# Partition-major model and MLP width in a two-layer decode kernel: long weight runs, strided weight columns, x and result in column form

## The chip, the cores and the metric

The kernel runs on one core of a Trainium2 chip. The time is the device time of one execution in microseconds (us), as the median of several executions; the profile's span, from its first to its last instruction, is some 2 us shorter than that time. Every timed kernel was run beside the kernel before, on the same chip. In the views, PE is the matmul engine and PEld its weight loads, DVE and ACT are the vector and the scalar engine, and SPq is the sequencer that issues the loads and stores of the one queue.

## The reference

One token passes twice through attention over the last 4,096 cached positions (32 heads of 192) and then through an MLP block. All tensors are bf16. The model width D is 640, the MLP width F is 1,536. Cut to what matters:

```python
def _A_ref(x, k_cache, v_cache, wq, wo):        # x: [1, 1, 640]
    q = (x @ wq)                                # wq: [640, 32 * 192]
    p = softmax(q k^T * 192 ** -0.5)            # k, v: the last 4096 positions of each head
    return (p v) @ wo                           # wo: [32 * 192, 640]

def _B_ref(x, w1, w2, w3, w4):                  # one token: the shifted part (w1, w2) is zero
    x1 = x
    h2 = gelu(layernorm(x1) @ w3) @ w4          # w3: [640, 1536], w4: [1536, 640]
    return x1 + h2

x = A_x
for _ in range(2):
    x = x + _A_ref(layernorm(x), ...)
    x = x + _B_ref(layernorm(x), ...)
```

## The kernel before

The kernel is a stream of 1.5 MB loads (a head of K or V at a time), all on one DMA queue, into 11 buffers ("cells") of 12 KB per partition. It keeps vectors as columns: D = 640 is a tile of 128 partitions by 5 columns. Which d stands where is the subject of the change. Before, column n holds d = 128 n + p on partition p:

```python
def load_wq(layer, kc):
    nc.sync.dma_start(wq_sb[:, kc, :], A_wq[kc * P:(kc + 1) * P, :])

def load_w3(layer):
    src = B_w3.rearrange("(k p) f -> p k f", p=P)                 # runs of one row, 3,072 B
    ...
def load_w4(layer):
    pairs = B_w4.rearrange("(k p two) n -> p k (two n)", p=P, two=2)  # runs of two rows, 2,560 B
    ...
# attention's output projection: 128 neighbouring columns of wo are the weights
nc.tensor.matmul(y_ps[:, n:n + 1], lhsT=wo_t[:, k * D + n * P:k * D + (n + 1) * P], rhs=oT[:, k:k + 1], ...)
# MLP: every second column of w3, 128 neighbouring columns of w4
f0 = 2 * P * (fc // 2) + fc % 2
nc.tensor.matmul(hp[:, i:i + 1], lhsT=w3[kc][:, f0:f0 + 2 * P - 1:2], rhs=xc[:, kc:kc + 1], ...)
nc.tensor.matmul(y2_ps[:, n:n + 1], lhsT=w4[fc][:, n * P:(n + 1) * P], rhs=hT[:, fc:fc + 1], ...)
# the end: turn [128, 5] into [5, 128], store five runs of 256 B
nc.tensor.transpose(row_ps[:, :], x4[:, :], Eq[:].rearrange("p j b -> p (j b)"))
nc.vector.tensor_copy(o_fin, row_ps[:])
nc.sync.dma_start(out.rearrange("a b (n p) -> (a b n) p", p=P), o_fin)
```

Every such matmul has one column as its moving operand, and with it goes a weight load of 128 x 128 (104 ns in the trace, overlapped, so that a pair of load and matmul starts every 27 ns). When layer 1 begins, 9 of the 11 cells hold data that is kept from layer 0. The first two V loads of layer 1 must therefore wait for the cells of w3 and w4 of layer 0.

Of the kernel before, what the change touches and what calls it, by code (L numbers as in the profile page):

```python
# [17 lines left out]
P = 128  # L18
# [17 lines left out]
def kernel(  # L36
# [37 lines left out]
    NA = Dh // 32  # L74
    NKX = 6
    NKEEP, NCELL = 7, 11
    WARM = 66



# [1 line left out]
    assert NA * D + FREE - 2 * VW <= FREE  # L82

    W3C, W4C = FREE // F, FREE // D
    assert W4C % 2 == 1 and W4C < NF
    GROUPS = [[list(range(h, h + QH)) for h in range(0, H, QH)] for _ in range(2)]
    GROUPS[0].reverse()

# [32 lines left out]

    def load_x():

        x_bf = wx_sb[0:ND, 4 * P:5 * P]
        nc.sync.dma_start(x_bf, A_x.rearrange("a b (n p) -> (a b n) p", p=P))
        return x_bf

    def load_k(layer, h):
# [23 lines left out]
            V, i = kx, i - (FREE - VN)  # L152
        return V[:, i:i + n]

    def load_wq(layer, kc):
        nc.sync.dma_start(wq_sb[:, kc, :], A_wq[kc * P:(kc + 1) * P, :])
        return wq_sb

    def load_wo(layer, c):
# [9 lines left out]
    def load_w3(layer):  # L169

        t = take(("w3", layer))
        src = B_w3.rearrange("(k p) f -> p k f", p=P)
        n = W3C if layer == 0 else W3C // 2
        for k in range(0, W3C, n):
            nc.sync.dma_start(t[:, k * F:(k + n) * F].rearrange("p (k f) -> p k f", f=F), src[:, k:k + n, :])
        if layer == 0:
            nc.sync.dma_start(wx_sb[:, 0:(ND - W3C) * F].rearrange("p (k f) -> p k f", f=F), src[:, W3C:, :])
        return ([t[:, k * F:(k + 1) * F] for k in range(W3C)]
                + [wx_sb[:, k * F:(k + 1) * F] for k in range(ND - W3C)])

    def load_w4(layer):

        t = take(("w4", layer))
        blocks = [t[:, k * D:(k + 1) * D] for k in range(W4C)]
        x0 = (ND - W3C) * F
        blocks += [wx_sb[:, x0 + k * D:x0 + (k + 1) * D] for k in range(NF - W4C)]
        pairs = B_w4.rearrange("(k p two) n -> p k (two n)", p=P, two=2)
        ones_ = B_w4.rearrange("(k p two) n -> p k two n", p=P, two=2)
        h = W4C // 2
        n = h if layer == 0 else h // 2  # L190
        for k in range(0, h, n):
            nc.sync.dma_start(t[:, 2 * k * D:2 * (k + n) * D].rearrange("p (k n) -> p k n", k=n), pairs[:, k:k + n, :])
        nc.sync.dma_start(blocks[2 * h], ones_[:, h, 0, :])
        if layer == 0:
            nc.sync.dma_start(blocks[2 * h + 1], ones_[:, h, 1, :])
            rest = NF // 2 - h - 1
            nc.sync.dma_start(wx_sb[:, x0 + D:x0 + D + 2 * rest * D].rearrange("p (k n) -> p k n", k=rest),
                              pairs[:, h + 1:, :])
        return blocks

    LOADERS = {"x": load_x, "k": load_k, "v": load_v, "wq": load_wq, "wo": load_wo, "w3": load_w3, "w4": load_w4}
# [39 lines left out]
        seq.append(("w4", layer))  # L241
        return seq

    stream = [("wq", 0, 0), ("x",)] + [("wq", 0, kc) for kc in range(1, ND)] + layer_stream(0) + layer_stream(1)
    pos = [0]

    def need(*key):
# [59 lines left out]
    for i in range(WARM):  # L307
        nc.tensor.matmul(warm_ps[:], lhsT=Eq[:, 0, :], rhs=Eq[:, 0, :], start=(i == 0), stop=(i == WARM - 1))

    x_rf = wx_sb[0:ND, 6 * P:8 * P].bitcast(F32)  # L310
    nc.vector.tensor_copy(x_rf, x_bf)
    xT = const.tile([P, ND], F32, name="xT0")
    xT_ps = psm.tile([P, ND], F32, tag="psm")
    nc.tensor.transpose(xT_ps[:, :], x_rf, ident[0:ND, 0:ND])
    rs0 = const.tile([P, 1], F32, name="rs0")
    nc.vector.tensor_scalar(out=xT[:], in0=xT_ps[:], scalar1=1.0, scalar2=None, op0=ALU.mult,
                            op1=ALU.add, accum_out=rs0[:, 0:1])


# [60 lines left out]
    def qproj_steps(c, xc, part=None, row=None):  # L380


        held = {}
        n = QT if part is None else QT // 2
        t0 = c * QT + (part or 0) * n

        def project():
            need("wq", 0, ND - 1)
            if row is not None:
                N = QC // 2  # L390
                qr_ps = psm.tile([33, N], F32, tag="psm")
                for kc in range(ND):
                    for i in range(2):
                        nc.tensor.matmul(  # L394
                            qr_ps[32 * i:32 * i + 1, :], lhsT=xc[:, kc:kc + 1],
                            rhs=wq_sb[:, kc, t0 * P + i * N:t0 * P + (i + 1) * N],
                            start=(kc == 0), stop=(kc == ND - 1))
                for i in range(2):
                    nc.scalar.copy(row[32 * i:32 * i + 1, :], qr_ps[32 * i:32 * i + 1, :])
                return  # L400
            qT_ps = psm.tile([P, n], F32, tag="psm")
            for tl in range(n):
                t = t0 + tl
                for kc in range(ND):
                    nc.tensor.matmul(  # L405
                        qT_ps[:, tl:tl + 1], lhsT=wq_sb[:, kc, t * P:(t + 1) * P], rhs=xc[:, kc:kc + 1],
                        start=(kc == 0), stop=(kc == ND - 1))
            held["q"] = qT_ps

        def spread():  # L410
            if row is not None:
                qT_ps = psm.tile([P, n], F32, tag="psm")
                for tl in range(n):
                    i, j = divmod(tl, n // 2)
                    nc.tensor.matmul(qT_ps[:, tl:tl + 1], lhsT=row[:, j * P:(j + 1) * P],
                                     rhs=Eq[0:33, i, 0:1], start=True, stop=True)
                held["q"] = qT_ps
            Xq = big.tile([P, n, 4], BF16, name="Xq")
            nc.vector.tensor_tensor(  # L419
                out=Xq[:], in0=held["q"][:, :].unsqueeze(2).broadcast_to([P, n, 4]),  # L420
                in1=maskq[:, :].unsqueeze(1).broadcast_to([P, n, 4]), op=ALU.mult)
            held["x"] = Xq

        def repeat():
            Qrep_ps = psm.tile([P, 4 * n], F32, tag="psm")
            nc.tensor.matmul(Qrep_ps[:], lhsT=Lb[:], rhs=held["x"][:].rearrange("p t b -> p (t b)"),  # L426
                             start=True, stop=True)
            held["r"] = Qrep_ps

        def block():  # L430
            nh = n * P // Dh
            h0 = 4 * (t0 - c * QT) // NCOL
            diag = Qblk[:, c % 2].rearrange("p (h r) -> p h r", h=QH)[:, h0:h0 + nh, 0:QHEAD]
            nc.vector.tensor_tensor(
                out=diag.rearrange("p h (f x) -> p h f x", x=QW)[:, :, :, 0:NM],
                in0=held["r"][:, :].rearrange("p (h f) -> p h f", h=nh).unsqueeze(3).broadcast_to([P, nh, NCOL, NM]),
                in1=blkm[:, :].unsqueeze(1).unsqueeze(1).broadcast_to([P, nh, NCOL, NM]), op=ALU.mult)

        return project, spread, repeat, block
# [149 lines left out]
    def out_proj(layer, *terms):  # L589
# [3 lines left out]
        for i, (c, oT, n, k) in enumerate(order):  # L593
            wo_t = need("wo", layer, c)
            nc.tensor.matmul(
                y_ps[:, n:n + 1], lhsT=wo_t[:, k * D + n * P:k * D + (n + 1) * P], rhs=oT[:, k:k + 1],
                start=(i == 0), stop=(i == len(order) - 1))
        for c, _ in terms:
            if (layer, c) == (0, 0):
# [26 lines left out]

    def turn_row(acc):
        y_ps = psm.tile([P, ND], F32, tag="psm")
        N = D // 2
        for n in range(ND):  # L630
            a, b = n * P, (n + 1) * P
            for i in range(2):
                lo_, hi = max(a, i * N), min(b, (i + 1) * N)
                if lo_ < hi:
                    nc.tensor.matmul(y_ps[lo_ - a:hi - a, n:n + 1], lhsT=acc[:, lo_ - i * N:hi - i * N],
                                     rhs=ident[0:33, 32 * i:32 * i + 1], start=True, stop=True)
        return y_ps

    def attention(layer, x_cur, rs_cur, x_new, z_new, rs_new, ss_new):
# [218 lines left out]
    def mixer(layer, x_cur, z, rs_cur, ss_cur, x_new, rs_new):  # L858
# [33 lines left out]
        for ks in kcs:  # L892
            for half, hp in enumerate(h_ps):
                order = ([(i, kc) for kc in ks for i in range(HF)] if ks is kcs[0] else
                         [(i, kc) for i in range(HF) for kc in ks])
                for j, (i, kc) in enumerate(order):
                    fc = half * HF + i
                    f0 = 2 * P * (fc // 2) + fc % 2
                    nc.tensor.matmul(
                        hp[:, i:i + 1], lhsT=w3[kc][:, f0:f0 + 2 * P - 1:2], rhs=xc[:, kc:kc + 1],  # L900
                        start=(ks is kcs[0] and j == 0), stop=(ks is kcs[-1] and j == len(order) - 1))
        give(("w3", layer))
        for half, hp in enumerate(h_ps):
# [20 lines left out]
        y2_ps = psm.tile([P, ND], F32, tag="psm")  # L924
        fcs = list(range(NF))
        if layer == 1:
            n = W4C // 4 * 2
            fcs = fcs[:n] + fcs[W4C:] + fcs[n:W4C]
        order = [(n, fc) for fc in fcs for n in range(ND)]
        for i, (n, fc) in enumerate(order):  # L930
            nc.tensor.matmul(
                y2_ps[:, n:n + 1], lhsT=w4[fc][:, n * P:(n + 1) * P], rhs=hT[:, fc:fc + 1],
                start=(i == 0), stop=(i == len(order) - 1))
        give(("w4", layer))
        if rs_new is None:
# [12 lines left out]
    attention(1, x2, rs2, x3, z[1], zs[2], zs[3])  # L948
    mixer(1, x3, z[1], zs[2], zs[3], x4, None)

    row_ps = psm.tile([ND, P], out.dtype, tag="psm")
    nc.tensor.transpose(row_ps[:, :], x4[:, :], Eq[:].rearrange("p j b -> p (j b)"))
    o_fin = Lb[0:ND, :]
    nc.vector.tensor_copy(o_fin, row_ps[:])
    nc.sync.dma_start(out.rearrange("a b (n p) -> (a b n) p", p=P), o_fin)


# [28 lines left out]
```

## Time and profile before

| what | value | view |
|---|---|---|
| time | 525.22 us, median of 3 (524.87 to 526.0) | results |
| span | 522.9 us | page |
| DMA | 415 GB/s; one queue has 99.0% of the engines' time | page |
| PE, DVE busy | 63%, 56% | page |

The lines of the page for the kernel before. The GB/s row has 40 slices of the span, 13.1 us each.

```profile
span 522.9 us, 9589 instructions
...
GB/s 345 429 424 425 423 426 427 423 424 423 427 421 428 424 422 428 423 423 423 423 399 398 388 425 427 424 424 423 426 423 424 426 423 426 421 427 425 420 410 237
DMA packets 23949, 217.08 MB, mean 415 GB/s; under 512 B 2532, under 2 KB 3044, under 8 KB 8420
```

The stream runs at some 424 GB/s nearly throughout; slices 20 to 22 (261 to 300 us), around the change of layers, are lower. So what is not hidden under the stream is there, at the start and at the end. The layer boundary before, from the timeline (start, duration, engine, line, operation, count, and in brackets the idle time before it and what ended it):

```profile
285.28 0.78 PE L899 MATMUL V_ps<-xc,cell_2751 128*128 128x1 bf16 x24
...
285.92 0.78 PE L899 MATMUL O_ps<-xc,cell_2751 128*128 128x1 bf16 x24
...
286.73 0.33 SPq L143 DMA_DIRECT2D cell_3122<-in_A_v_cache_dram  x1
...
288.32 1.43 PE L931 MATMUL y_ps<-hT,cell_2863 128*128 128x1 bf16 x45 [1.30 <-DVE gu L907]
...
289.78 0.33 SPq L143 DMA_DIRECT2D cell_3124<-in_A_v_cache_dram  x1
...
294.19 0.33 SPq L130 DMA_DIRECT2D cell_3126<-in_A_k_cache_dram  x1
```

Here w3's matmuls (line 899) end and the first V load of layer 1 is issued at once, w4's matmuls (line 931) on their buffer end and the second one is issued. The spacing of matmul pairs is the group's time less one matmul, over the count less one: (780 - 165) / 23 = 27 ns for w3, (1430 - 165) / 44 = 29 ns for w4, whose group holds one pause of 0.1 us (its other pairs start 27 ns apart).

What the sequencer waited for before it issued that first V load, from the view of its waits (line, who released it, us in total, times, longest):

```profile
SPq L143 <- PE O_ps L899: 3.0, 1, 3.0
```

The same stretch before, in the view by windows (start:end, length, busy time and count of PE, PEld, DVE, ACT and GpSimd, granted clock of PE, DMA share, GB/s):

```profile
285.00:290.00 5.00, 3.70 (x116) 3.55 (x117) 2.61 (x19) 1.91 (x8) 0.00 (x0) 0.50 1.01 371
290.00:295.00 5.00, 4.18 (x84) 2.96 (x87) 1.07 (x8) 0.30 (x2) 0.00 (x0) 0.50 1.02 430
```

And the end before, from the timeline:

```profile
519.20 0.81 PE L931 MATMUL y_ps<-hT,cell_5535 128*128 128x1 bf16 x25
520.04 0.16 DVE L936 TENSOR_TENSOR x_213<-base,y_ps 128x5 bf16<-128x5 f32 x1 [1.14 <-PE y_ps L931]
...
520.26 0.27 PE L952 MATMUL row_ps<-Eq,x_213 128*5 128x128 bf16 x1 [0.26 <-DVE x_213 L936]
520.57 0.21 DVE L954 COPY Lb<-row_ps 5x128 bf16<-5x128 bf16 x1 [0.36 <-PE row_ps L952]
520.81 0.30 SPq L955 DMA_DIRECT2D out_dram<-Lb  x1
```

From the last add to the issue of the store are 0.77 us, from there to the end of the span 2.1 us.

### The profile page before, as it was taken

Reading aid. Unit: us, or ns where it says so; the run is one execution under the profiler, and the core shown is the slowest. Engines: PE = TensorE matmul, PEld = TensorE weight load, DVE = VectorE, ACT = ScalarE, POOL = GpSimd, SP = SyncE. Lnnn points to the kernel's source line nnn. Section 1 sums busy time; section 2 is a strip of 40 time slices with the busy share of each in tenths; the row PEclk is TensorE's granted clock in tenths of the full one; section 3 lists DMA queues with packets and bytes.
Section 4 is the critical chain, followed back from the end, with each engine's and each line's share of the span. In section 5 each row is a group of like instructions: output and inputs, shape, how many; then the busy total and the mean of one; then the engine's idle time right before and its main releaser. Section 6 shows DMA issues by size and latency. Waiting matters only on the chain.

```text
span 522.9 us, 9589 instructions
## 1 busy us (share of the span) xinstructions
PE 330.3 (63%) x4146; PEld 195.5 (37%) x4146; DVE 294.6 (56%) x589; ACT 49.5 (9%) x175; POOL 4.0 (1%) x16
## 2 busy tenths in 40 slices
PE   2057668666665566767655866667675666647675
PEld 2023334333332333434333544334343333425344
DVE  2067656666574664556624264766576866654722
ACT  1000101010010100001011101001010101001011
POOL 2000000000000000000000000000000000000000
PEclk9995656567677776576555567657787865766755
DMA  8999999999999999999999999999999999999996
GB/s 345 429 424 425 423 426 427 423 424 423 427 421 428 424 422 428 423 423 423 423 399 398 388 425 427 424 424 423 426 423 424 426 423 426 421 427 425 420 410 237
DMA packets 23949, 217.08 MB, mean 415 GB/s; under 512 B 2532, under 2 KB 3044, under 8 KB 8420
## 3 DMA queue, kind: packets, MB, share of 16 engines
q1 hardware_dynamic: 23908, 216.48, 99.0%
q8 instruction: 32, 0.52, 0.4%
q14 instruction: 9, 0.07, 0.0%
HBM read 216.47 MB, written 0.00 MB: 414 GB/s over the span
## 4 chain that ended last, share of the span: by engine, by line
DMA 43%; PE 27%; DVE 25%; issue 2%; ACT 2%; SPq 1%; DVEq 0%; ACTq 0%
PE ST_ps L451 11%; DVE cell_3304 L375 9%; PE O_ps L567 8%; DVE cell_277 L375 8%; DMA cell_1925<-in_A_k_cache_dram 6%; DMA cell_4933<-in_A_k_cache_dram 5%; DMA cell_1629<-in_A_k_cache_dram 5%; DMA cell_1329<-in_A_k_cache_dram 5%; DMA cell_4637<-in_A_k_cache_dram 5%; DMA cell_5324<-in_A_v_cache_dram 5%; DMA cell_275<-in_A_k_cache_dram 4%; DVE o_sb L574 2%; DMA cell_2478<-in_A_v_cache_dram 2%; DMA cell_2690<-in_A_v_cache_dram 2%; DMA cell_5423<-in_B_w_dram 2%
## 5 line engine op out<-in xcount | busy, mean ns | idle before, releaser
L451 PEld LDWEIGHTS <-Qblk 128*16 128x16 bf16 x1536 | 86.1, 113 | 178.6 <-issue 151.1
L451 PE MATMUL ST_ps<-cell_277,Qblk 128*16 128x256 bf16 x600 | 70.1, 392 | 50.9 <-DVE cell_277 L375 34.3
L574 DVE STREAM_TRANSPOSE o_sb<-O_ps 128x384 f32<-128x384 f32 x64 | 37.2, 582 | 112.4 <-PE O_ps L567 112.3
L451 PE MATMUL ST_ps<-cell_3304,Qblk 128*16 128x256 bf16 x600 | 67.3, 382 | 43.5 <-DVE cell_3304 L375 28.3
L567 PEld LDWEIGHTS <-PT 128*2 128x2 bf16 x1024 | 47.2, 102 | 21.8 <-issue 11.3
L510 DVE STREAM_TRANSPOSE o_sb<-o_sb 128x256 bf16<-128x256 bf16 x16 | 7.1, 445 | 34.1 <-ACT o_sb L505 25.0
L582 ACT ACTIVATE oT<-oT_ps,rl 32x6 bf16<-32x6 f32 x40 | 10.3, 258 | 163.5 <-PE oT_ps L581 157.1
L581 PEld LDWEIGHTS oT_ps<-o_sb,Lq 128*32 128x32 f32 x160 | 13.2, 145 | 19.9 <-issue 16.1
L581 PE MATMUL oT_ps<-o_sb,Lq 128*32 128x6 f32 x160 | 13.9, 196 | 10.4 <-DVE o_sb L574 9.9
L587 ACT ACTIVATE oT<-oT_ps,rl 32x6 bf16<-32x6 f32 x24 | 6.2, 258 | 108.4 <-PE ST_ps L451 93.7
L405 PE MATMUL qT_ps<-xc,wq_sb 128*128 128x1 bf16 x210 | 7.2, 165 | 13.4 <-DMA wq_sb<-in_A_wq_dram 12.5
L419 DVE TENSOR_TENSOR Xq<-qT_ps,maskq 128x24 bf16<-128x24 f32 (+1 forms) x18 | 2.8, 157 | 18.3 <-PE qT_ps L405 18.3
L521 PE MATMUL PT_ps<-o_sb,Eq 128*32 128x32 bf16 x256 | 7.2, 237 | 9.2 <-DVE o_sb L510 4.0
L394 PE MATMUL qr_ps<-wq_sb,xc 128*1 128x384 bf16 x90 | 12.8, 433 | 0.0
L521 PEld LDWEIGHTS <-Eq 128*32 128x32 bf16 x256 | 5.5, 111 | 18.9 <-issue 18.8
L405 PEld LDWEIGHTS <-wq_sb 128*128 128x128 bf16 x210 | 6.8, 104 | 14.8 <-DMA wq_sb<-in_A_wq_dram 13.6
L502 ACT COPY nb_sb<-nb_ps 128x1 f32<-128x1 f32 x16 | 2.5, 159 | 97.6 <-PE nb_ps L499 97.6
L526 PE MATMUL l_ps<-lh,ones 128*128 128x4 f32 x32 | 8.5, 336 | 4.9 <-ACT PT L524 4.9
L499 PEld LDWEIGHTS nb_ps<-ones,o_sb 1*128 1x128 f32 x32 | 7.6, 292 | 7.4 <-issue 5.5
L526 PEld LDWEIGHTS l_ps<-lh,ones 128*128 128x128 f32 x32 | 7.1, 275 | 7.5 <-ACT PT L524 7.1
L499 PE MATMUL nb_ps<-ones,o_sb 1*128 1x1 f32 x32 | 8.9, 345 | 1.5 <-DVE o_sb L491 1.5
L426 PE MATMUL Qrep_ps<-Xq,Lb 128*128 128x24 bf16 (+1 forms) x18 | 3.2, 179 | 10.4 <-DVE Xq L419 10.1
(376 smaller groups left out, 533.2 us busy)
## 6 DMA issues: line engine op xcount, KB each, us to landing
wq_sb<-in_A_wq_dram SPq DMA_DIRECT2D x5, 1536.0 KB, 12.7
cell_275<-in_A_k_cache_dram SPq DMA_DIRECT2D x1, 1536.0 KB
cell_309<-in_A_k_cache_dram SPq DMA_DIRECT2D x1, 1536.0 KB, 26.4
cell_346<-in_A_k_cache_dram SPq DMA_DIRECT2D x1, 1536.0 KB, 27.1
cell_376<-in_A_k_cache_dram SPq DMA_DIRECT2D x1, 1536.0 KB
cell_444<-in_A_k_cache_dram SPq DMA_DIRECT2D x1, 1536.0 KB, 30.8
cell_503<-in_A_v_cache_dram SPq DMA_DIRECT2D x1, 1536.0 KB, 30.8
cell_505<-in_A_k_cache_dram SPq DMA_DIRECT2D x1, 1536.0 KB, 30.8
```

The costliest lines, as they stand in the source:

```text
L375: nc.vector.transpose(Tu, Ku[:, :, q * NY:(q + 1) * NY])
L394: nc.tensor.matmul(qr_ps[32 * i:32 * i + 1, :], lhsT=xc[:, kc:kc + 1], rhs=wq_sb[:, kc, t0 * P + i * N:t0 * P + (i + 1) * N], start=(kc == ...
L405: nc.tensor.matmul(qT_ps[:, tl:tl + 1], lhsT=wq_sb[:, kc, t * P:(t + 1) * P], rhs=xc[:, kc:kc + 1], start=(kc == 0), stop=(kc == ND - 1))
L451: nc.tensor.matmul(ST_ps[r:r + QW, :].rearrange("p (g i) -> p g i", g=ng), lhsT=Q[:, n, :], rhs=T4[:, :, f, :, t], start=(hq == 0 and n == ...
L499: nc.tensor.matmul(nb_ps[:], lhsT=held["w"], rhs=ones[0:1, 0:1], start=True, stop=True)
L510: nc.vector.transpose(held["PrT"], held["Pr"])
L521: nc.tensor.matmul(PT_ps[32 * m:32 * (m + 1), :, :, ng * q:ng * (q + 1)], lhsT=Eq[:, q, :], rhs=src[:, m:QW:NM], start=True, stop=True)
L526: nc.tensor.matmul(l_ps[:], lhsT=ones[:], rhs=held["lh"][:], start=True, stop=True)
L567: nc.tensor.matmul(O_ps[r:r + 2, :], lhsT=PT[:, hq, 2 * i:2 * i + 2], rhs=v_pair(V, h, 2 * i * Dh, 2 * Dh), start=(i < 4), stop=(i >= NB - 4))
L574: nc.vector.transpose(o_sb[:], O_ps.rearrange("p (e a c) -> p e c a", e=2, c=NA))
L581: nc.tensor.matmul(oT_ps[r, :], lhsT=Lq[:], rhs=o_sb[:, e, :, e], start=(e == 0), stop=(e == 1))
L582: nc.scalar.activation(oT[r, :], oT_ps[r, :], ACTF.Copy, scale=rl[r, 0:1])
```

## The change

Column n now holds d = 5 p + n, and the MLP's columns f = 12 p + fc ("partition-major"). Every partition's part of wq, w3 and w4 is then one long run in memory, x is loaded straight into columns, and the result is stored straight from them. The price is in the weights: the 128 columns that belong to one output column are no longer neighbours.

```diff
-        nc.sync.dma_start(x_bf, A_x.rearrange("a b (n p) -> (a b n) p", p=P))
+        nc.sync.dma_start(x_bf, A_x.rearrange("a b (p n) -> (a b p) n", n=ND))
...
-        nc.sync.dma_start(wq_sb[:, kc, :], A_wq[kc * P:(kc + 1) * P, :])
+        src = A_wq.rearrange("(p k) n -> p k n", k=ND)
+        k = slice(0, 1) if part == 0 else slice(1, ND)
+        nc.sync.dma_start(wq_sb[:, k, :], src[:, k, :])
...
-        src = B_w3.rearrange("(k p) f -> p k f", p=P)
+        src = B_w3.rearrange("(p k) f -> p (k f)", k=ND)
...
-        pairs = B_w4.rearrange("(k p two) n -> p k (two n)", p=P, two=2)
+        src = B_w4.rearrange("(p k) n -> p (k n)", k=NF)
...   (x: the cast and the transpose at the start go)
-                y_ps[:, n:n + 1], lhsT=wo_t[:, k * D + n * P:k * D + (n + 1) * P], rhs=oT[:, k:k + 1],
+                y_ps[:, n:n + 1], lhsT=wo_t[:, k * D + n:(k + 1) * D:ND], rhs=oT[:, k:k + 1],
...   (turn_row, which turns the accumulated row into columns: 12 matmuls become 10; warm-up matmuls: 66 become 63)
-                        hp[:, i:i + 1], lhsT=w3[kc][:, f0:f0 + 2 * P - 1:2], rhs=xc[:, kc:kc + 1],
+                        hp[:, i:i + 1], lhsT=w3[kc][:, fc::NF], rhs=xc[:, kc:kc + 1],
...
-                y2_ps[:, n:n + 1], lhsT=w4[fc][:, n * P:(n + 1) * P], rhs=hT[:, fc:fc + 1],
+                y2_ps[:, n:n + 1], lhsT=w4[fc][:, n::ND], rhs=hT[:, fc:fc + 1],
...
-    row_ps = psm.tile([ND, P], out.dtype, tag="psm")
-    nc.tensor.transpose(row_ps[:, :], x4[:, :], Eq[:].rearrange("p j b -> p (j b)"))
-    o_fin = Lb[0:ND, :]
-    nc.vector.tensor_copy(o_fin, row_ps[:])
-    nc.sync.dma_start(out.rearrange("a b (n p) -> (a b n) p", p=P), o_fin)
+    nc.sync.dma_start(out.rearrange("a b (p n) -> (a b p) n", n=ND), x4[:])
```

In bytes between the columns of one weight load, w3 goes from 4 to 24 and w4 and wo from 2 to 10. wq's columns stay neighbours.

More of the change, by code (lines that the diff above doesn't have):

```diff
@@ L76 @@
     NKEEP, NCELL = 7, 11
-    WARM = 66
+    WARM = 63
     VC, VP, VX, VW, VN = 3, 2, 4, 20 * Dh // 2, NKX * Dh
@@ L84 @@
     W3C, W4C = FREE // F, FREE // D
-    assert W4C % 2 == 1 and W4C < NF
+    W4P = 4, W4C - 5, 1
+    assert W4C > 5 and W4C < NF
     GROUPS = [[list(range(h, h + QH)) for h in range(0, H, QH)] for _ in range(2)]
@@ L122, in load_x @@
     def load_x():
-        x_bf = wx_sb[0:ND, 4 * P:5 * P]
-        nc.sync.dma_start(x_bf, A_x.rearrange("a b (n p) -> (a b n) p", p=P))
+        x_bf = wx_sb[:, 4 * P:4 * P + ND]
+        nc.sync.dma_start(x_bf, A_x.rearrange("a b (p n) -> (a b p) n", n=ND))
         return x_bf
@@ L153, in v_pair, with load_wq @@
         return V[:, i:i + n]
-    def load_wq(layer, kc):
-        nc.sync.dma_start(wq_sb[:, kc, :], A_wq[kc * P:(kc + 1) * P, :])
+    def load_wq(layer, part):
+        src = A_wq.rearrange("(p k) n -> p k n", k=ND)
+        k = slice(0, 1) if part == 0 else slice(1, ND)
+        nc.sync.dma_start(wq_sb[:, k, :], src[:, k, :])
         return wq_sb
@@ L171, in load_w3 @@
         t = take(("w3", layer))
-        src = B_w3.rearrange("(k p) f -> p k f", p=P)
+        src = B_w3.rearrange("(p k) f -> p (k f)", k=ND)
         n = W3C if layer == 0 else W3C // 2
         for k in range(0, W3C, n):
-            nc.sync.dma_start(t[:, k * F:(k + n) * F].rearrange("p (k f) -> p k f", f=F), src[:, k:k + n, :])
+            nc.sync.dma_start(t[:, k * F:(k + n) * F], src[:, k * F:(k + n) * F])
         if layer == 0:
-            nc.sync.dma_start(wx_sb[:, 0:(ND - W3C) * F].rearrange("p (k f) -> p k f", f=F), src[:, W3C:, :])
+            nc.sync.dma_start(wx_sb[:, 0:(ND - W3C) * F], src[:, W3C * F:])
         return ([t[:, k * F:(k + 1) * F] for k in range(W3C)]
@@ L186, in load_w4 @@
         blocks += [wx_sb[:, x0 + k * D:x0 + (k + 1) * D] for k in range(NF - W4C)]
-        pairs = B_w4.rearrange("(k p two) n -> p k (two n)", p=P, two=2)
-        ones_ = B_w4.rearrange("(k p two) n -> p k two n", p=P, two=2)
-        h = W4C // 2
-        n = h if layer == 0 else h // 2
-        for k in range(0, h, n):
-            nc.sync.dma_start(t[:, 2 * k * D:2 * (k + n) * D].rearrange("p (k n) -> p k n", k=n), pairs[:, k:k + n, :])
-        nc.sync.dma_start(blocks[2 * h], ones_[:, h, 0, :])
+        src = B_w4.rearrange("(p k) n -> p (k n)", k=NF)
+        k = 0
+        for n in (W4C,) if layer == 0 else W4P:
+            nc.sync.dma_start(t[:, k * D:(k + n) * D], src[:, k * D:(k + n) * D])
+            k += n
         if layer == 0:
-            nc.sync.dma_start(blocks[2 * h + 1], ones_[:, h, 1, :])
-            rest = NF // 2 - h - 1
-            nc.sync.dma_start(wx_sb[:, x0 + D:x0 + D + 2 * rest * D].rearrange("p (k n) -> p k n", k=rest),
-                              pairs[:, h + 1:, :])
+            nc.sync.dma_start(wx_sb[:, x0:x0 + (NF - W4C) * D], src[:, W4C * D:])
         return blocks
@@ L242, in layer_stream @@
         return seq
-    stream = [("wq", 0, 0), ("x",)] + [("wq", 0, kc) for kc in range(1, ND)] + layer_stream(0) + layer_stream(1)
+    stream = [("wq", 0, 0), ("x",), ("wq", 0, 1)] + layer_stream(0) + layer_stream(1)
     pos = [0]
@@ L308 @@
         nc.tensor.matmul(warm_ps[:], lhsT=Eq[:, 0, :], rhs=Eq[:, 0, :], start=(i == 0), stop=(i == WARM - 1))
-    x_rf = wx_sb[0:ND, 6 * P:8 * P].bitcast(F32)
-    nc.vector.tensor_copy(x_rf, x_bf)
     xT = const.tile([P, ND], F32, name="xT0")
-    xT_ps = psm.tile([P, ND], F32, tag="psm")
-    nc.tensor.transpose(xT_ps[:, :], x_rf, ident[0:ND, 0:ND])
     rs0 = const.tile([P, 1], F32, name="rs0")
-    nc.vector.tensor_scalar(out=xT[:], in0=xT_ps[:], scalar1=1.0, scalar2=None, op0=ALU.mult,
+    nc.vector.tensor_scalar(out=xT[:], in0=x_bf, scalar1=1.0, scalar2=None, op0=ALU.mult,
                             op1=ALU.add, accum_out=rs0[:, 0:1])
@@ L387, in project @@
         def project():
-            need("wq", 0, ND - 1)
+            need("wq", 0, 1)
             if row is not None:
@@ L628, in turn_row @@
         y_ps = psm.tile([P, ND], F32, tag="psm")
-        N = D // 2
         for n in range(ND):
-            a, b = n * P, (n + 1) * P
             for i in range(2):
-                lo_, hi = max(a, i * N), min(b, (i + 1) * N)
-                if lo_ < hi:
-                    nc.tensor.matmul(y_ps[lo_ - a:hi - a, n:n + 1], lhsT=acc[:, lo_ - i * N:hi - i * N],
-                                     rhs=ident[0:33, 32 * i:32 * i + 1], start=True, stop=True)
+                nc.tensor.matmul(y_ps[64 * i:64 * (i + 1), n:n + 1], lhsT=acc[:, n::ND],
+                                 rhs=ident[0:33, 32 * i:32 * i + 1], start=True, stop=True)
         return y_ps
@@ L897, in mixer @@
                     fc = half * HF + i
-                    f0 = 2 * P * (fc // 2) + fc % 2
                     nc.tensor.matmul(
-                        hp[:, i:i + 1], lhsT=w3[kc][:, f0:f0 + 2 * P - 1:2], rhs=xc[:, kc:kc + 1],
+                        hp[:, i:i + 1], lhsT=w3[kc][:, fc::NF], rhs=xc[:, kc:kc + 1],
                         start=(ks is kcs[0] and j == 0), stop=(ks is kcs[-1] and j == len(order) - 1))
@@ L926, in mixer @@
         if layer == 1:
-            n = W4C // 4 * 2
+            n = W4P[0]
             fcs = fcs[:n] + fcs[W4C:] + fcs[n:W4C]
```

## The prediction

> **What bounds the kernel.** The page shows a span of 522.9 us, one queue with 99.0% of the DMA engines' time, 415 GB/s, DMA busy 9 tenths or more in 38 of 40 slices; PE is busy 63%, DVE 56%. Compute is exposed in three places of the timeline: the start (the first K transpose waits until 25.76 us for wq and a K block), the layer boundary (284 to 290 us), and the end, where the last w3 piece lands at 515.96, GELU gives hT at 518.7, 40 matmuls end at 520.0, a transpose and a copy follow until 520.8, and the output DMA ends the span at 522.9.
>
> **What the change does, costed.**
> 1. *Long runs.* Bytes stay. Packets in the trace took 466 ns for 12,288 B (26.4 B/ns), 125 ns for 3,072 B (24.6), 106 ns for 2,560 B (24.2), 57 ns for 1,280 B (22.5): about 9 ns each beyond the bytes. The Trainium skill, "DMA: Bandwidth & Descriptors", "Why small descriptors are slow (HBM only)", states a fixed overhead per packet; the trace agrees. w3 goes from 1,152 packets to 512, w4 from about 1,540 to 640, wq from 640 to 256: 120 fewer per engine, estimated 1.1 us (0.6 layer 0's MLP weights, 0.35 layer 1's, 0.15 wq). K, V and wo, over 90% of the bytes, do not change.
> 2. *x and result in column form.* At the start a cast and a transpose go, but PE waits there for wq until 22.08 us anyway: 0. At the end transpose and copy go, 520.2 to 520.8: 0.6 us, all critical. The output becomes 128 runs of 10 B, not 5 of 256 B: estimated +0.2.
> 3. *Strided weight columns.* w3 columns go from a step of 4 B to 24 B, w4 and wo from 2 B to 10 B. Pairs of weight load and matmul now run at 27 to 31 ns. The Trainium skill, "SBUF — State Buffer", on cachelines, says that steps beyond 16 B pay. No bf16 weight load with such a step is in this trace; if w3's pair became 54 ns, the end gets 24 x 27 ns = 0.65 us longer, w4's 40 matmuls perhaps 0.4, and the release of w3's buffer at the boundary (V load issued at 286.73) comes 1.3 us later, of which half might starve the queue. Even odds, at half that size.
> 4. Turning the accumulated row (12 matmuls, 2.27 us) becomes 10 narrower ones, hidden under the stream.
>
> **Sum.** Without a stride penalty -1.1 - 0.6 + 0.2 = -1.5 us; with the full one about 0. I predict 524.2 us, 8 in 10 between 522.4 and 525.9. Faster by over 2%: 1%; within 2%: 98.5%; slower: 0.5%.
>
> **What the profile would show.** (1) Fewer packets under 8 KB; slices 20 to 22 (399, 398, 388 GB/s) and 38 above their values now. (2) No instruction between the last add of x and the output DMA; wrong if the output DMA takes over 0.5 us longer to land. (3) The spacing of w3's and w4's matmul pairs at the end and at 285 us: 27 ns if strides are free, 50 or more if not. The first K transpose should still start near 25.7 us.
>
> **What would make it wrong.** A weight load with a 24 B step far slower than doubled; runs of 48 KB making engines uneven, so that the slowest of 16 ends later; 128 tiny packets at either end costing a microsecond or more; or long runs raising the rate by more than the per-packet cost, which would bring 521 to 522 us.

## The result, and the profile after

The changed kernel takes 528.37 us (median of 4, 528.16 to 529.61) against 525.05 us for the kernel before in the runs beside it. A ratio here is the mean time of one kernel's fast runs over that of the other's of the same rounds, so not quite the ratio of the medians quoted. It is 1.0067 (95% interval 1.0053 to 1.0082), or 3.5 us slower. A difference in us below is the ratio less one times 525.2 us, unless a trace is named.

The page of the changed kernel:

```profile
span 526.4 us, 9602 instructions
...
GB/s 359 421 427 422 422 428 425 423 428 420 427 422 426 424 422 428 424 422 425 421 420 338 388 421 432 419 427 421 425 423 424 425 425 422 425 425 426 421 410 162
DMA packets 22217, 217.08 MB, mean 412 GB/s; under 512 B 2720, under 2 KB 2976, under 8 KB 6816
```

The packets under 8 KB are fewer, as intended, and slice 20 is up from 399 to 420 GB/s. But slice 21 is down from 398 to 338, and slices 22 (388) and 38 (410) are what they were. Its layer boundary, from the timeline:

```profile
285.18 1.52 PE L888 MATMUL V_ps<-xc,cell_2746 128*128 128x1 bf16 x24
...
286.56 1.54 PE L888 MATMUL O_ps<-xc,cell_2746 128*128 128x1 bf16 x24
...
288.13 0.33 SPq L144 DMA_DIRECT2D cell_3115<-in_A_v_cache_dram  x1
...
289.92 1.92 PE L920 MATMUL y_ps<-hT,cell_2858 128*128 128x1 bf16 x45 [1.12 <-DVE gu L896]
...
291.87 0.33 SPq L144 DMA_DIRECT2D cell_3117<-in_A_v_cache_dram  x1
...
296.32 0.33 SPq L131 DMA_DIRECT2D cell_3119<-in_A_k_cache_dram  x1
```

w3's pairs now take (1520 - 197) / 23 = 58 ns, w4's (1920 - 178) / 44 = 40 ns. The first V load is issued 1.40 us later than before, the second 2.09, the first K load 2.13. The sequencer's wait for w3's matmuls was 3.0 us long and is now 5.1:

```profile
SPq L144 <- PE V_ps L888: 5.1, 1, 5.1
```
The windows of the changed kernel show what the queue did meanwhile:

```profile
285.00:290.00 5.00, 3.88 (x65) 3.83 (x66) 1.80 (x15) 1.28 (x6) 0.00 (x0) 0.50 0.55 186
290.00:295.00 5.00, 4.18 (x99) 3.87 (x102) 1.61 (x12) 0.92 (x5) 0.00 (x0) 0.50 0.95 398
```

In 285 to 290 us the DMA engines were 55% busy and moved 186 GB/s instead of 371. PE's granted clock was 0.50 in these windows of both kernels, and from 513 to 522 us too, so the slower pairs are not a matter of the clock. And the end:

```profile
521.11 1.14 PE L920 MATMUL y_ps<-hT,cell_5532 128*128 128x1 bf16 x25
522.28 0.16 DVE L925 TENSOR_TENSOR x_207<-base,y_ps 128x5 bf16<-128x5 f32 x1 [1.66 <-PE y_ps L920]
522.47 0.35 SPq L940 DMA_DIRECT2D out_dram<-x_207  x1
```

The last add is 2.24 us later than before. From it to the issue are 0.19 us (0.77 before), from the issue to the end of the span 3.9 us (2.1 before). The spans differ by 2.24 - 0.58 + 1.84 = 3.5 us.

How far the stream was ahead or behind is counted from the DMA packets of the traces: bytes moved by a given time, against the kernel before, in us at 424 GB/s.

| by (us) | changed kernel | all steps mended | w3's step alone on the kernel before | two halves |
|---|---|---|---|---|
| 285 | 1.08 ahead | 1.21 ahead | 0.44 ahead | 1.13 ahead |
| 290 | 1.03 behind | 0.76 ahead | 1.12 behind | 0.36 ahead |
| 305 | 1.08 behind | 0.26 ahead | 1.03 behind | 2.18 behind |
| 500 | 1.11 behind | 0.31 ahead | 1.10 behind | 2.18 behind |

The last three columns are experiments, below (a_all_contig, b_w3_step24, a_split). The changed kernel had gained its microsecond by 285 us, lost two in five, and then carried the microsecond that it was behind to 500 us. Traces of like kernels scatter by some 0.4 us here: b_out10 and b_w3_step24, which have the loads of the kernel before, stand 0.32 and 0.44 ahead of it at 285 us, and b_out10 0.07 behind at 305.

### The profile page after: what moved, and what is told of

Same layout as the page of the kernel before. It is cut to its first block, busy times and chain, and to the rows that moved or that the text cites. A ratio compares the mean times of both kernels' runs of the same rounds, so it can differ in the third digit from the quotient of the medians.

```text
span 526.4 us, 9602 instructions
## 1 busy us (share of the span) xinstructions
PE 327.7 (62%) x4157; PEld 198.1 (38%) x4157; DVE 294.9 (56%) x587; ACT 49.4 (9%) x175; POOL 4.0 (1%) x16
## 4 chain that ended last, share of the span: by engine, by line
DMA 46%; PE 25%; DVE 24%; issue 2%; ACT 1%; SPq 0%; DVEq 0%; ACTq 0%
PE ST_ps L445 9%; DVE cell_3297 L369 9%; DVE cell_268 L369 8%; PE O_ps L561 7%; DMA cell_1916<-in_A_k_cache_dram 6%; DMA cell_5274<-in_A_v_cache_dram 6%; DMA cell_1620<-in_A_k_cache_dram 5%; DMA cell_4926<-in_A_k_cache_dram 5%; DMA cell_1320<-in_A_k_cache_dram 5%; DMA cell_4630<-in_A_k_cache_dram 5%; DMA cell_266<-in_A_k_cache_dram 4%; DMA cell_2239<-in_A_k_cache_dram 3%; DMA cell_2512<-in_A_v_cache_dram 2%; DMA cell_5383<-in_A_wo_dram 2%; DVE o_sb L568 2%; DMA cell_2685<-in_A_v_cache_dram 2%
## 5 line engine op out<-in xcount | busy, mean ns | idle before, releaser
L561 PEld LDWEIGHTS <-PT 128*2 128x2 bf16 x1024 | 45.1, 100 | 22.3 <-issue 11.2
L388 PE MATMUL qr_ps<-wq_sb,xc 128*1 128x384 bf16 x90 | 11.4, 396 | 0.0
```

What stands on the lines that cost most here:

```text
L388: nc.tensor.matmul(qr_ps[32 * i:32 * i + 1, :], lhsT=xc[:, kc:kc + 1], rhs=wq_sb[:, kc, t0 * P + i * N:t0 * P + (i + 1) * N], start=(kc == ...
L561: nc.tensor.matmul(O_ps[r:r + 2, :], lhsT=PT[:, hq, 2 * i:2 * i + 2], rhs=v_pair(V, h, 2 * i * Dh, 2 * Dh), start=(i < 4), stop=(i >= NB - 4))
```

## The experiments

The theory after the result: the loss has three parts, the 10 B runs of the output, w3's 24 B step and the 10 B step of w4 and wo, and the steps cost twice, once at the end and once at the boundary, where the stream's next loads wait for w3's and w4's buffers. The rival: the new loads themselves (runs of 48 KB, fewer and larger transfers) starve the queue or leave the 16 engines uneven.

Twelve kernels were run. Kernels that read neighbours where strided columns belong, or the reverse, compute another function. Most passed the comparison with the reference all the same, within its tolerance, so passing says nothing about them. They tell costs only.

| run | median us | ratio to before (95%) | us over before, by the ratio | by the medians |
|---|---|---|---|---|
| changed kernel | 528.37 | 1.0067 (1.0053 to 1.0082) | +3.5 | +3.32 |
| a_w3_contig | 527.9 | 1.0043 (1.0025 to 1.006) | +2.3 | +2.69 |
| a_w4wo_contig | 527.75 | 1.0046 (1.0029 to 1.0062) | +2.4 | +2.45 |
| a_all_contig | 525.94 | 1.0009 (0.9991 to 1.0027) | +0.5 | +0.73 |
| a_L0_contig | 526.23 | 1.0027 (1.0009 to 1.0045) | +1.4 | +1.23 |
| a_L1_contig | 527.25 | 1.0043 (1.0028 to 1.0058) | +2.3 | +2.25 |
| a_row_out | 528.67 | 1.006 (1.004 to 1.008) | +3.2 | +3.46 |
| a_split | 530.31 | 1.0096 (1.008 to 1.0111) | +5.0 | +5.01 |
| b_w3_step24 | 527.12 | 1.0027 (1.0006 to 1.0048) | +1.4 | +1.91 |
| b_out10 | 526.64 | 1.003 (1.0014 to 1.0046) | +1.6 | +1.34 |
| width_only | 527.12 | 1.0036 (1.0023 to 1.0049) | +1.9 | +2.12 |
| b_triples | 525.27 | 1.0001 (0.999 to 1.0012) | +0.1 | +0.27 |
| b_step_ladder | 525.78 (one run, state unknown) | none | none | none |

Names beginning with a_ are the changed kernel with an edit, b_ and width_only the kernel before with one. Three batches, in this order: the first four below, the next four, the last four. The last column is a run's median less that of the kernel before in its batch (525.21, 525.30 and 525.00 us; 525.05 for the changed kernel). In the first batch two of the seven runs of the kernel before took 526.26 and 526.78 us. They raise its mean, and so the differences by the ratio are 0.3 to 0.5 us lower than those by the medians in that batch. The expectations below were written with differences of medians ("0.5 us, with all mended 2.4"). A part that is worth less than half a microsecond is not resolved here.

The edits are shown shortened, to the lines that carry the test.

### a_w3_contig: w3 read as neighbours

```diff
-   lhsT=w3[kc][:, fc::NF]
+   lhsT=w3[kc][:, fc * P:(fc + 1) * P]
```

> The changed kernel, all loads and everything else kept, only w3's weight columns read as 128 neighbours (2 B step) instead of every 12th (24 B step). Wrong result on purpose. Theory (the step is the cost): the spacing of w3's matmul pairs falls from about 60 ns to 27 ns, the first V load of layer 1 is issued about 1.5 us earlier at the boundary, the DMA gap there shrinks to what it was before, the end gets 0.65 us shorter: 1.5 to 2.2 us faster than the changed kernel, about 526.4. Rival (the new shape of the loads starves the queue or makes the engines uneven): only the end gets shorter, about 527.8, and the DMA gap at 285 to 290 us stays.

Measured: 1.3 us less than the changed kernel (0.6 by the medians), short of the 1.5 to 2.2 expected. The pairs were back at 27 ns, the first V load was issued at 286.72 us (288.13 in the changed kernel), and the stream was no longer behind at 290 us (0.29 us ahead). From 285 to 290 us it moved 278 GB/s: more than the changed kernel's 186, but not the 371 of the kernel before, whose stream was 1.2 us less far on at 285 us.

```profile
285.00:290.00 5.00, 3.69 (x105) 3.73 (x106) 2.61 (x19) 1.90 (x8) 0.00 (x0) 0.50 0.73 278
```

So most of the gap did come from the step, not from the shape of the loads. The end did not follow. In this kernel's timeline the last projection waited for data:

```profile
519.64 0.96 PE L920 MATMUL y_ps<-hT,cell 128*128 128x1 bf16 x20 [2.31 <-DMA cell<-in_B_w_dram]
```

A piece of w4 landed late although the stream as a whole was early. The packets of this trace show how: from 519.4 to 521.1 us they follow each other one at a time, eight of 5,120 B and eight of 1,280 B, as from one DMA engine that has its share left when the others are done. So uneven engines, which the rival names, did tell at the end of this run. a_all_contig has the same loads and its last piece landed at 519.2 us, so the loads alone do not make it; what does is not shown.

### a_all_contig: w3, w4 and wo read as neighbours

The edit above, and in addition:

```diff
-   lhsT=w4[fc][:, n::ND]
+   lhsT=w4[fc][:, n * P:(n + 1) * P]
-   lhsT=wo_t[:, k * D + n:(k + 1) * D:ND]
+   lhsT=wo_t[:, k * D + n * P:k * D + (n + 1) * P]
```

> The same, with w4's and wo's columns read as neighbours too (2 B step for 10 B). Wrong result on purpose; only the loads and the output form of the change are left. Theory: another 0.4 to 0.8 us off, about 525.7; the pairs of w4 and wo fall from 40 to 28 ns. What is left over the kernel before is then the 10-byte output less the gain of the long runs. Rival: 527 or more.

Measured: +0.5 us over the kernel before, 3.0 us less than the changed kernel (+0.7 and 2.6 by the medians). All of the change's loads, x and output form are still in it. The total is near the 525.7 us expected; the step from the run before is larger than the 0.4 to 0.8 expected, because that run had fallen short. The rival needed 527 us or more and falls. The steps cost 2.6 to 3.0 us in all.

### a_row_out: the result as two rows

```diff
-    nc.sync.dma_start(out.rearrange("a b (p n) -> (a b p) n", n=ND), x4[:])
+    for i in range(2):
+        for n in range(ND):
+            nc.tensor.matmul(row_ps[32 * i:32 * i + 1, n::ND], lhsT=x4[:, n:n + 1],
+                             rhs=Eq_flat[:, 64 * i:64 * (i + 1)], start=True, stop=True)
+    nc.vector.tensor_copy(o_fin[0:1, :], row_ps[0:1, :])
+    nc.scalar.copy(o_fin[32:33, :], row_ps[32:33, :])
+    ...   (two stores of 640 B)
```

> The changed kernel with the result turned into two rows of 320 by ten small matmuls and two copies, and stored as two runs of 640 B (correct result). Theory (128 runs of 10 B take 3.9 us from issue to the end of the span, 5 of 256 B took 2.1): from issue to the end about 2.1 us, turning costs 0.7 us, so 1.1 us faster than the changed kernel, about 527.3. Rival (the output is not at fault, it waits for the uneven engines): no faster than the changed kernel, 528.4 or more.

Measured: no gain that the intervals can tell (+3.2 us over before, +3.5 for the changed kernel). The timeline says why:

```profile
523.03 0.16 DVE L925 TENSOR_TENSOR x<-base,y_ps 128x5 bf16<-128x5 f32 x1 [1.65 <-PE y_ps L920]
...
524.52 0.68 SPq L950 DMA_DIRECT2D out_dram<-kx  x2
```

From the last add to the first issue were 1.49 us: the turn cost 1.3 us more than no turn (0.19), not 0.7. From there to the end of the span (527.1) were 2.6 us instead of 3.9. The store was cheaper, as the theory has it, and the turn ate the gain. As a test of the total it is inconclusive; b_out10 settles it.

### b_w3_step24: the step alone, on the kernel before

```diff
-   lhsT=w3[kc][:, f0:f0 + 2 * P - 1:2]
+   lhsT=w3[kc][:, fc::NF]
```

> The kernel before, all loads kept, only w3's columns read with a 24 B step. Wrong result on purpose. Theory: pairs at about 60 ns, first V load of layer 1 issued 1.5 us later, a DMA gap at 286 to 290 us, 1.5 to 2 us slower than the kernel before: 526.8. Rival: at most 0.7 us slower, at the end alone, 525.8, and no more gap at the boundary.

Measured: +1.4 us by the ratio, a little under the 1.5 to 2 expected, and +1.9 by the medians, within them. The interval of the ratio (0.3 to 2.5 us) does not exclude the rival's 0.7, so the trace has to decide. The loads are those of the kernel before, the first V load is issued 1.59 us later than there, and the gap at the boundary, which the rival denied, is there:

```profile
288.32 3.57 SPq L143 DMA_DIRECT2D cell<-in_A_v_cache_dram  x2
```

The stream goes from 0.44 us ahead at 285 us to 1.12 behind at 290 and stays there (table above). The step alone makes the gap.

### b_out10: the output alone, on the kernel before

```diff
-    nc.tensor.transpose(row_ps[:, :], x4[:, :], ...)
-    nc.vector.tensor_copy(o_fin, row_ps[:])
-    nc.sync.dma_start(out.rearrange("a b (n p) -> (a b n) p", p=P), o_fin)
+    nc.sync.dma_start(out.rearrange("a b (p n) -> (a b p) n", n=ND), x4[:])
```

> The kernel before with only the end changed: no transpose and no copy, the result stored straight from its column tile as 128 runs of 10 B (values in a wrong order on purpose). Theory: the last add to the issue of the output DMA falls from 0.77 to 0.2 us, issue to the end of the span rises from 2.1 to 3.9 us; net 1.2 us slower than the kernel before, about 526.4. Rival (the output form costs nothing or gains, as the failed row-form run may suggest): 524.7 to 525.3.

Measured: +1.6 us (+1.3 by the medians). Its span is 524.3 us, and the end of its timeline is:

```profile
520.31 0.16 DVE L936 TENSOR_TENSOR x<-base,y_ps 128x5 bf16<-128x5 f32 x1 [1.14 <-PE y_ps L931]
520.50 0.36 SPq L951 DMA_DIRECT2D out_dram<-x  x1
```

So 0.19 us from add to issue, and 3.8 us from issue to end, against 0.77 and 2.1: 1.2 us more in all, as expected. (The rest of the span's 1.5 us is a last add that came 0.27 us later.) In the trace the 128 packets of 10 B start within 0.2 us, at 521.4 to 521.5 us; the rest of the time comes after them. In the kernel before, the five packets of 256 B start at 521.6 us and the span ends 1.2 us later; here it ends 2.8 us after the last packet. Whether it is the size of the runs, their number or the number of engines that makes the difference, these runs do not separate.

### a_w4wo_contig: w4 and wo as neighbours, w3's step kept

```diff
-   lhsT=w4[fc][:, n::ND]
+   lhsT=w4[fc][:, n * P:(n + 1) * P]
-   lhsT=wo_t[:, k * D + n:(k + 1) * D:ND]
+   lhsT=wo_t[:, k * D + n * P:k * D + (n + 1) * P]
```

> The changed kernel with w4's and wo's columns read as neighbours, w3's step of 24 B kept (wrong result on purpose). With w3 alone mended the gain was 0.5 us, with all mended 2.4. Theory A (the costs of the two steps add up, and the run with w3 mended was held by a late piece of w4): about 1.2 us of chain at the end and 0.4 before the boundary go, 526.9 to 527.3. Theory B (10 B steps are the main cost, 24 B steps nearly free): 526.4 or less, and the boundary gap small.

Measured: 1.1 us less than the changed kernel by the ratios; the median, 527.75 us, lies above the range of theory A and far above theory B's 526.4. Mended one at a time the steps give 1.3 and 1.1 us, together 3.0 (0.6, 0.9 and 2.6 by the medians): more together than apart. The intervals of both single runs touch that of the changed kernel, but every run of either (at most 528.14 us) is below every run of it (at least 528.16), and their pairs (27 ns for w3's, and for w4's and wo's) show what was taken away. Neither step is free.

### b_step_ladder: one weight load at nine steps

```diff
+   if g == 0:    lhsT = w3[kc][:, 0:127 * 1 + 1:1]       # 2 B
+   elif g == 1:  lhsT = w3[kc][:, 0:127 * 2 + 1:2]       # 4 B
+   ...           steps of 6, 8, 10, 12, 16, 20, 24 and again 2 B, six matmuls each, layer 0 only
```

> The kernel before with layer 0's w3 columns read at steps of 2, 4, 6, 8, 10, 12, 16, 20, 24 and again 2 B, six matmuls each (wrong result on purpose); a look at the duration of one weight load and at the pair spacing. Theory (a load pays for each step into another 16 B line): 2 and 4 B 104 ns, 8 B at most 120, 10 B 131, 24 B 155, with 16 to 24 B alike. Rival (it pays by the distance in bytes): 16, 20 and 24 B still rise.

Measured, the weight loads in the timeline of PE, in the order of the ladder:

```profile
285.07 0.42 PEld L905 LDWEIGHTS <-cell 128*128 128x128 bf16 x6
285.41 0.24 PEld L907 LDWEIGHTS <-cell 128*128 128x128 bf16 x6
285.57 0.24 PEld L909 LDWEIGHTS <-cell 128*128 128x128 bf16 x6
285.74 0.28 PEld L911 LDWEIGHTS <-cell 128*128 128x128 bf16 x6
285.93 0.32 PEld L913 LDWEIGHTS <-cell 128*128 128x128 bf16 x6
286.17 0.37 PEld L915 LDWEIGHTS <-cell 128*128 128x128 bf16 x6
286.44 0.47 PEld L917 LDWEIGHTS <-cell 128*128 128x128 bf16 x6
286.80 0.45 PEld L919 LDWEIGHTS <-cell 128*128 128x128 bf16 x6
287.15 0.46 PEld L921 LDWEIGHTS <-wx_sb 128*128 128x128 bf16 x6
287.50 0.27 PEld L923 LDWEIGHTS <-wx_sb 128*128 128x128 bf16 x6
```

The first group (2 B) holds the wait for its matmul's operand, so the last (2 B again) and the second (4 B) stand for free loads. From the start of one group to the next, over six:

| step | 4 B | 6 B | 8 B | 10 B | 12 B | 16 B | 20 B | 24 B |
|---|---|---|---|---|---|---|---|---|
| ns a pair | 27 | 28 | 32 | 40 | 45 | 60 | 58 | 58 |

It is flat to 6 B, rises from 8 B, and is flat again from 16 B on. That is the shape of a cost for each access to another 16 B line, and the rival (a cost that grows with distance) falls. Counted in such lines, 128 columns touch some 64 at 8 B, 80 at 10 B, 96 at 12 B and 128 from 16 B on, and each of these pairs comes to about 0.5 ns a line (32, 40, 45 and 58 to 60 ns); below that the pairs stay at 27 to 28 ns. One load took 117 ns at 8 B and 130 at 10 B, as expected. The expectation that one load stays at 155 ns for 24 B was a little low in this kernel: the mean of those six is 166 ns.

### a_split: layer 1's first V load in two halves

```diff
+   # the load goes into w3's own tile, in two halves; each waits only for the readers of its half
+   cut = FREE // 2,
-   kcs = [cell, rest] if layer == 0 else ...
+   kcs = [cell[:2], cell[2:], rest] if layer == 0 else ...
```

> The changed kernel, steps kept, but the first V load of layer 1 goes into w3's buffer in two halves, and w3's matmuls of layer 0 run so that its first half is free after 24 of them (correct result). Theory (the DMA queue runs dry at the boundary because that load waits for w3's buffer): the first half is issued about 1.4 us earlier, the gap at 285 to 290 us shrinks by about that, and the stream runs 1 us or more ahead of the changed kernel from there to the end: 527.2. Rival (the gap is not what sets the end): 528.2 or more.

Measured: a miss, +5.0 us over before, 1.5 us slower than the changed kernel. The first half was issued at 286.58 us, 1.55 us earlier, as meant, and its windows show the queue fuller at once and emptier afterwards:

```profile
285.00:290.00 5.00, 3.89 (x67) 3.84 (x68) 1.73 (x15) 1.39 (x6) 0.00 (x0) 0.50 0.79 287
290.00:295.00 5.00, 4.18 (x100) 3.87 (x102) 1.53 (x11) 0.81 (x5) 0.00 (x0) 0.50 0.93 306
295.00:300.00 5.00, 5.00 (x109) 3.19 (x105) 0.36 (x2) 0.46 (x2) 0.00 (x0) 0.64 0.87 318
```

In 290 to 295 us it moved 306 GB/s where the changed kernel moved 398. The first K load was issued at 296.21 us, as late as in the changed kernel (296.32), since it waits for the layer's scores. So an earlier first load moved the gap rather than closing it. What must come earlier is the whole chain of releases, as it does in a_L0_contig, below. By its number the rival of this run (528.2 or more) was met. But it had the gap not matter, and here the stream stood 1.1 us further behind than the changed kernel's at 500 us and the time was 1.5 us longer, so the two still went together. Why the stream lost a further microsecond by 305 us (2.18 behind, table above) is open; no run here tells it.

### a_L0_contig and a_L1_contig: the steps mended in one layer

```diff
+   lhsT=(neighbours if layer == 0 else strided)     # a_L0_contig: w3, w4 and wo
+   lhsT=(neighbours if layer == 1 else strided)     # a_L1_contig
```

> The changed kernel with w3, w4 and wo read as neighbours in layer 0 only; layer 1 and so the end keep their steps (wrong result on purpose). Theory (about half of the steps' cost is a later start of layer 1's loads at the boundary, which the stream carries to the end): first V load of layer 1 issued about 2 us earlier, the stream 1.3 us further by 305 us, and the time 0.8 to 1.5 us less than the changed kernel's, 526.9 to 527.6. Rival (only the end counts, the queue makes up for the boundary): within 0.4 us of 528.4.

> The mirror image: neighbours in layer 1 only, steps kept in layer 0. Theory: the gap at 285 to 290 us and the stream's delay stay as in the changed kernel, the chain from the last V block to the last add gets about 1.2 us shorter: 527.0 to 527.6. With the run before it the two gains should add up to the 2.4 us of all steps mended. Rival: if it gains 2 us or more, the boundary costs nothing.

Measured: layer 0 alone gives back 2.1 us, layer 1 alone 1.3, both 3.0 (2.1, 1.1 and 2.6 by the medians). So they nearly add up, and the larger part is layer 0's, which the end of the kernel never sees directly. With layer 0 mended the stream was 0.40 us ahead at 305 us where the changed kernel's was 1.08 behind, 1.5 us further (1.3 expected), and so it stayed to 500 us. The V load was issued at 286.30 us with layer 0 mended and at 288.49 with layer 1 mended. The window 285 to 290 us, first of a_L0_contig:

```profile
285.00:290.00 5.00, 3.43 (x121) 3.34 (x118) 2.42 (x19) 1.91 (x8) 0.00 (x0) 0.50 0.83 315
```

and of a_L1_contig:

```profile
285.00:290.00 5.00, 4.15 (x64) 4.10 (x64) 1.54 (x12) 1.22 (x5) 0.00 (x0) 0.50 0.53 184
```

The rival of the first (the queue makes up for the boundary) falls. Layer 0's gain is above the 0.8 to 1.5 us expected: its time of 526.23 us is below the range. Layer 1's time of 527.25 us is within its range, and its rival (a gain of 2 us or more) falls. The profiled run of a_L1_contig was its slowest (528.43 us), so its window may look a little worse than usual.

### width_only: the MLP width alone

The kernel before, with w4 in the change's long runs and w3 at the 24 B step, and the model width left as it was (a correct result).

```diff
-   pairs = B_w4.rearrange("(k p two) n -> p k (two n)", p=P, two=2)
+   src = B_w4.rearrange("(p k) n -> p (k n)", k=NF)
-   lhsT=w3[kc][:, f0:f0 + 2 * P - 1:2]
+   lhsT=w3[kc][:, fc::NF]
```

> The kernel before with the MLP width alone laid out partition-major: w4 in long runs, w3's columns at a 24 B step, w4's and wo's columns neighbours, model width, x and output as before (correct result). Theory: as the run with w3's step alone (527.1), less at most 0.4 us for w4's longer runs: 526.6 to 527.1. Rival (the long runs earn their keep): 525.8 or less.

Measured: +1.9 us (527.12 us, at the upper edge of the range), no less than with w3's step alone (+1.4, intervals overlapping; the two medians are both 527.12). The longer runs of w4 show no gain in time here.

### b_triples: a candidate

```diff
-   pairs = B_w4.rearrange("(k p two) n -> p k (two n)", p=P, two=2)
+   src = B_w4.rearrange("(k p three) n -> p k (three n)", p=P, three=3)
-   f0 = 2 * P * (fc // 2) + fc % 2;        lhsT = w3[kc][:, f0:f0 + 2 * P - 1:2]
+   f0 = 3 * P * (fc // 3) + fc % 3;        lhsT = w3[kc][:, f0:f0 + 3 * P - 2:3]
```

> A candidate: the kernel before with the MLP width in threes instead of pairs: w3's columns at 6 B, a step that the ladder shows to be free (27 to 28 ns a pair), w4 in runs of 3,840 B, fewer packets, everything else as before (correct result). Theory: the packets save at most 0.3 us, part of it lost at the boundary: 524.9 to 525.3, not to be told from the kernel before. Rival (long runs help where they cost nothing): 524.5 or less.

Measured: ratio 1.0001 over five rounds, not to be told from the kernel before. It keeps w3's step at 6 B, which the ladder shows to be nearly free, and has fewer packets, and it costs nothing and gains nothing. No version that beats both kernels was found.

## Why the prediction was wrong

The prediction said 524.2 us within 522.4 to 525.9; 528.37 was measured. One path of runs leads from the kernel before to the changed one, a part at a time: output form +1.6 us (b_out10); then loads and x -1.1 (from b_out10 to a_all_contig); then steps +3.0 (from a_all_contig to the changed kernel). The three add up by construction. By the medians they are +1.3, -0.6 and +2.6. The middle term is a difference between two batches whose intervals overlap, and the spans of the two profiled runs differ by 0.2 us only (524.3 and 524.1); it could be zero. Against the prediction's terms the steps missed by most, 2.1 to 2.5 us; the output missed by 1.6 to 2.0.

- **Bound by DMA, exposed at start, boundary and end: right.** The first K transpose started at 25.73 us (25.76 before). What was missed is how the boundary works as a chain: wo's, w3's and w4's matmuls, then the scores, each release a buffer that the queue is waiting for.
- **Long runs, -1.1 us: the size in the stream was right, what it is worth was not.** Of the 1.1, 0.75 us (wq and layer 0's MLP weights) was to come by 285 us. The stream was 1.08 us ahead then, of which 0.3 to 0.4 may be scatter (above). But the next loads wait for buffers, not for the queue, so most of being early there only lengthens the gap: with all steps mended, 1.21 us ahead at 285 us had become 0.26 at 305. The sign named for it failed in part: slice 20 rose, slice 21 fell to 338 GB/s, slices 22 and 38 stayed.
- **Output, "estimated +0.2", with -0.6 for the transpose and copy: a step that failed.** The saving was there, 0.77 to 0.19 us from add to issue. The store of 128 runs of 10 B took 3.9 us from issue to the end of the span against 2.1, so +1.8 where +0.2 stood. The net is a loss of 1.2 us by the traces and 1.6 by the times (alone on the kernel before; interval 0.7 to 2.4), not a gain of 0.4. The prediction had named this risk ("128 tiny packets at either end costing a microsecond or more") and its sign ("over 0.5 us longer to land"). The estimate had looked at the time of packets, which is 0.2 us; the cost comes after them. The Trainium skill, "DMA: Bandwidth & Descriptors", section "Anatomy of one DMA — SWDGE (gpsimd) path", says of the GpSimd path that most of a DMA's fixed cost is the target memory's write receipt and that HBM is the heaviest target. This store is issued from SP, and a wait after the last packet (2.8 us here, 1.2 before) would fit that. That it is the receipt, no run shows, and the page's fixed cost does not say why 128 small runs wait 1.6 us longer than five.
- **Steps, "even odds, at half that size": the step that failed by most, its mechanism right, its size wrong.** The prediction put the full penalty at about 1.5 us, and its 524.2 holds some 0.5 of that (525.2 - 1.5 + 0.5). Measured are 3.0 (2.6 by the medians). w3's pair went to 58 ns (54 supposed). wo's pairs, 27 to 39 ns (30 in 0.94 us became 30 in 1.32 at the boundary), were named and then left out of the sum, and so were w4's at the boundary. And "of which half might starve the queue" was too little: layer 0's steps alone cost 2.1 us (a_L0_contig), more than those at the end (1.3, a_L1_contig). The Trainium skill, "SBUF — State Buffer", on cachelines, named the mechanism, and the ladder bears it out. The even odds on it were one mistake and the size the other: with the penalty in full the prediction's sum was still about 0.
- **The turned row hidden:** no run tests it alone; it is in a_all_contig, which is 0.5 to 0.7 us over the kernel before with all that is left of the change.

## What to carry to other kernels

A layout that makes loads longer pays for them where the data is used: at runs of 2.5 to 3 KB there was an estimated 9 ns a packet to gain, while a pair of weight load and matmul whose columns stand 16 B or more apart took twice as long (58 to 60 for 27 ns), and 6 B cost nearly nothing. In a kernel bound by its stream, look for the places where loads wait for buffers: matmuls that hold such a buffer can be on the critical path though their engine is idle for a third of the time, as here, and whatever the stream gained before that point can be lost there. Do not price a store by its packets alone: measure from its issue to the end.

## What the Trainium skill lacked or had wrong

- "SBUF — State Buffer", cachelines: it gives 8 bf16 (16 B) as how far one can step for free, and says in the same place that two hits a line are needed. For 128 x 128 weight loads the free range ended at 6 B (28 ns a pair against 27); 8 B, with its two hits, cost 32 ns, and 16 B had the full cost, 60 ns. So the hits a line are the better guide of the two, and two of them were nearly but not quite enough.
- "TensorE: Matmul & The Clock Gate", "LDWEIGHTS (loading the stationary operand)": its formula has the count of columns alone, 107 ns for 128, and the trace has 104 ns for neighbours. It has no term for the step; at 24 B the same load took 155 to 166 ns in the traces.
- "DMA: Bandwidth & Descriptors", specifications: it puts all transfers under 512 B in one class. Five runs of 256 B and 128 runs of 10 B, 1,280 B both, ended the span 1.2 and 2.8 us after their packets. No page gives the time from a small store's last packet to its end by the size or number of its runs.
